# A sentence's v moved, and the gate's product behind one more expert chunk, in a fused attention and expert kernel

## The chip, the cores and the metric

The kernel runs on one core of a Trainium2 chip. The metric is the device time of one execution in microseconds (us). TensorE (PE) multiplies matrices into PSUM, a small accumulator memory; VectorE (DVE), ScalarE (ACT) and GpSimd (POOL) work elementwise; SyncE (SP) only issues transfers (DMA). Each engine runs its own list of instructions in order, and waits at an instruction whose input or buffer is not ready. Transfers issued by POOL go through one queue (q0), those issued by SP through another (q1); both are served by the same 16 DMA engines. POOL's transfers convert from float32 to 16-bit numbers on the way, SP's do not.

## The reference

For each of 8 sentences: attention in 8 heads over 576 positions with head size 64, where a position sees itself and the 63 before it; then one expert network for the whole sentence, chosen by a gate.

```python
scores = scale * np.matmul(q, k.transpose(0, 1, 3, 2))
mask = (rel >= 0) & (rel < window)          # window 64
attn = softmax of the masked scores
x = attn @ v, heads side by side            # (8, 576, 512)
...
logits = x.mean(axis=1) @ w_gate            # one row per sentence
e = argmax(logits); gate_w = softmax(logits)[e]
out = gate_w * (np.maximum(x @ w1[e], 0.0) @ w2[e])
```

q, k, v are float32 (8, 8, 576, 64); w1 is (8, 512, 1024) and w2 (8, 1024, 512) in float32. The expert of a sentence is known only when its attention is done, and only then can its weights be loaded: per sentence 2 MB each of w1 and w2 as float32.

## The kernel before

A sentence `b` is two half-sentences (units) of four heads, so there are 16 units `t`. The main loop has one step per unit, from step 4 to step 19; units 0 to 3 and the first expert chunks stand ahead of it in a hand-written start. All instructions are recorded in program order, so the order of the code is the order on each engine.

In a step `t` PE turns q and k of the next unit (`transpose_qk`), computes scores of this unit in three pieces (`scores(t, c)`: ACT takes the exponential, DVE multiplies with the band's 0/1 mask in `mask_out`), multiplies with v (`values`, two pieces; the row sums come out as a 65th column, and DVE divides in `norm`), and turns the finished x of the unit before (`transpose_x`; ACT copies it to `xT` and takes the sums over the sentence as it does, DVE forms the gate's partial sums `gpart` of them). Between these stand chunks of the expert of an earlier sentence, called in portions by `experts(pace)`: eight up-chunks (`expert_up`, 8 matmuls into `php`, ReLU and gate weight on ACT into `hT`), then five down-chunks (`expert_down`, into `pso`, copied to `ob` by DVE or ACT, stored by SP).

PSUM is given out in four buffers in turn (`psum`, four of 4 KB per partition): a new product waits until whoever reads the product four allocations earlier is done.

At an even step the sentence before is complete. `next_gate` then issues the gate's product (`gl`, one small matmul with ones that adds over partitions), five small DVE instructions (`glog`, `gmx`, `graw`, `eidx`, `gnm`) that find the expert's number, and on POOL a register load of it, the load of w1, q and k of a later unit, w2, and the load of a later sentence's v. POOL holds one queue of this, in order. Two w1 buffers and two w2 buffers exist. The first two sentences' w1 is loaded in two halves, the first of which suffices for the first four up-chunks; the others whole.

v of a sentence is loaded by SP into one of three buffers (`load_v`), 36 blocks of 128 rows in (partition, block, 64) layout. To place it in time a one-element write by POOL goes ahead of it: a memset, which waits only for the buffer, or a copy of an element of some tile, which also waits for that tile. DVE casts v to 16 bits for each unit: `cast_part` "whole" into `va`, then "low" and "high", the same shifted by half a block, into `vb`; `cast_v` does all three.

In the kernel before, the fourth sentence's v (b = 3) comes in two transfers: 20 blocks in the start, 16 blocks at step 5 behind the landing of the second half of the second sentence's w1 (`load_rest`). The fifth's (b = 4) is issued at the end of step 5. Sentences 5 to 7 are issued in `next_gate` of steps 6, 8 and 10. SP's list holds the stores of `ob` as well; `ob` has ten buffers.

In an even step `t` from 6 on the order around the gate is: `transpose_x(t - 1)`, two pieces of scores with their masks held back, one expert chunk, the gate, the two masks, the cast of the next v ("whole"), one expert chunk, the third piece of scores, the gate's weight. At step 16, the last gate, there are no scores.

## Time and profile before

| | us |
|---|---|
| median of 3 runs | 225.32 (225.25 to 226.03) |
| the profiled execution | 225.92 |
| its span, first to last instruction | 224.0 |
| PE busy in the span | 201.1 (90%) |
| ACT busy | 134.2 (60%) |
| DVE busy | 128.6 (57%) |
| share of 16 DMA engines by q0 (POOL's) | 65.3% |
| share by q1 (SP's) | 28.9% |

The span is shorter than the execution's time by 1.9 us, which lie before the first and after the last instruction. Times in rows of the profile are counted from the span's start. A row of the timeline gives start, duration, engine, line, operation and tiles, how many instructions it merges, and in brackets how long the engine stood idle before it and what ended that. A row of the chain gives start, duration and what it was. DMA rows give a queue's packets, megabytes and the time that its packets took as a share of the 16 engines, or one issue's size and the us from issue to landing.

### The profile page before, as it was taken

Reading aid. Unit: us, or ns where it says so; the run is one execution under the profiler, and the core shown is the slowest. Engines: PE = TensorE matmul, PEld = TensorE weight load, DVE = VectorE, ACT = ScalarE, POOL = GpSimd, SP = SyncE. Lnnn points to the kernel's source line nnn. Section 1 sums busy time; section 2 is a strip of 40 time slices with the busy share of each in tenths; the row PEclk is TensorE's granted clock in tenths of the full one; section 3 lists DMA queues with packets and bytes.
Section 4 is the critical chain, followed back from the end, with each engine's and each line's share of the span. In section 5 each row is a group of like instructions: output and inputs, shape, how many; then the busy total and the mean of one; then the engine's idle time right before and its main releaser. Section 6 shows DMA issues by size and latency. Waiting matters only on the chain.

```text
span 224.0 us, 6996 instructions
## 1 busy us (share of the span) xinstructions
PE 201.1 (90%) x3012; PEld 141.4 (63%) x3012; DVE 128.6 (57%) x310; ACT 134.2 (60%) x221; POOL 39.1 (17%) x69
## 2 busy tenths in 40 slices
PE   7859759999799897999999999999999998999960
PEld 2437638856586556865696658775777567569520
DVE  2538696557866665576774769395939373330120
ACT  2275695964768464785769476968495656417300
POOL 7170161053000700034000700050002000200000
PEclk9976999999999999999999999999999999999995
DMA  5999899999999999999999999999956990699141
GB/s 69 243 256 246 149 157 219 242 251 235 257 225 203 236 223 244 230 288 217 244 227 277 218 231 235 250 264 219 246 141 113 212 266 5 97 225 263 52 136 41
DMA packets 34310, 45.64 MB, mean 204 GB/s; under 512 B 7136, under 2 KB 26720, under 8 KB 34272
## 3 DMA queue, kind: packets, MB, share of 16 engines
q0 software_dynamic: 14624, 26.22, 65.3%
q1 hardware_dynamic: 18704, 18.75, 28.9%
q8 instruction: 25, 0.41, 0.7%
q10 hardware_dynamic: 944, 0.16, 0.4%
q14 instruction: 13, 0.11, 0.1%
HBM read 61.90 MB, written 9.44 MB: 318 GB/s over the span
## 4 chain that ended last, share of the span: by engine, by line
PE 64%; DMA 12%; ACT 11%; DVE 6%; issue 2%; POOL 1%; POOLq 0%
PE php L570 26%; PE pso L584 20%; DMA w1t<-in_moe_w_dram 8%; PE tp L342 6%; ACT xT L470 5%; DMA kn<-in_k_dram 4%; PE op L425 4%; ACT hT L574 4%; PE sp L382 2%; PE pso L601 2%; ACT pt L397 2%; DVE x L441 1%; PE tp L462 1%; DVE vb L311 1%; PE gl L501 1%
## 5 line engine op out<-in xcount | busy, mean ns | idle before, releaser
L570 PE MATMUL php<-xT,w1t 128*128 128x288 f16 x512 | 70.0, 287 | 3.4 <-DMA w1t<-in_moe_w_dram 2.3
L574 ACT ACTIVATE hT<-php,gatew 128x576 f16<-128x576 f32 x64 | 47.2, 744 | 28.8 <-PE php L570 28.6
L570 PEld LDWEIGHTS <-w1t 128*128 128x128 f16 x512 | 56.0, 115 | 10.0 <-DMA w1t<-in_moe_w_dram 2.9
L584 PE MATMUL pso<-w2t,hT 128*128 128x512 f16 x256 | 60.2, 380 | 0.2
L397 ACT ACTIVATE pt<-sp 128x768 f16<-128x768 f32 x48 | 36.4, 817 | 7.5 <-PE sp L382 7.5
L584 PEld LDWEIGHTS <-hT 128*128 128x128 f16 x256 | 23.3, 98 | 26.1 <-issue 1.2
L311 DVE COPY ob<-pso 128x512 f32<-128x512 f32 x23 | 15.9, 690 | 22.9 <-PE pso L584 22.7
L441 DVE TENSOR_TENSOR x<-op,linv 128x640 f16<-128x640 f32 x32 | 26.4, 825 | 1.1
L404 DVE TENSOR_TENSOR pt<-pt,masks 128x768 f16<-128x768 f16 x42 | 22.6, 554 | 5.7 <-ACT pt L397 4.7
L355 ACT COPY dst<-tp 128x1152 bf16<-128x1152 bf16 x16 | 18.0, 1124 | 11.9 <-PE tp L342 11.7
L547 POOL DMA_DIRECT2D w1t<-in_moe_w_dram x6 | 4.4, 729 | 112.8 <-DVE pt L404 91.5
L470 ACT ACTIVATE xT<-tp 128x576 f16<-128x576 f16 x28 | 17.9, 646 | 9.2 <-PE tp L462 9.2
L425 PE MATMUL op<-vb,pt 128*64 128x65 f16 x320 | 16.2, 198 | 0.8 <-DVE ob L311 0.7
L311 DVE COPY vb<-va 64x1152 f16<-64x1152 f16 (+1 forms) x32 | 15.9, 498 | 0.5
L425 PEld LDWEIGHTS <-pt 128*64 128x64 f16 x640 | 13.9, 114 | 3.3 <-issue 2.4
L425 PE MATMUL op<-va,pt 128*64 128x65 f16 x320 | 15.9, 198 | 0.0
L382 PE MATMUL sp<-dst 64*64 64x128 bf16 (+1 forms) x672 | 14.2, 218 | 1.9 <-ACT dst L309 1.2
L382 PEld LDWEIGHTS <-dst 64*64 64x64 bf16 x672 | 10.3, 110 | 8.7 <-issue 4.5
L311 DVE CAST va<-vn 128x1152 f16<-128x1152 f32 x16 | 12.2, 763 | 6.2 <-DMA vn<-in_v_dram 6.1
L493 DVE SCALAR_TENSOR_TENSOR gpart<-wg,pooled,gpart 128x8 f32<-128x8 f32 x21 | 4.8, 226 | 18.4 <-ACT xT L470 18.1
L342 PE MATMUL tp<-ident,kn 128*64 128x128 bf16 x288 | 11.5, 227 | 1.9 <-DMA kn<-in_k_dram 1.9
L342 PEld LDWEIGHTS <-kn 128*64 128x64 bf16 x288 | 9.0, 113 | 6.0 <-issue 3.5
(74 smaller groups left out, 178.5 us busy)
## 6 DMA issues: line engine op xcount, KB each, us to landing
w2t<-in_moe_w_dram POOLq DMA_DIRECT2D x8, 1024.0 KB, 17.6
out_dram<-ob SPq DMA_DIRECT2D x31, 256.0 KB, 8.1
w1t<-in_moe_w_dram POOLq DMA_DIRECT2D x6, 1024.0 KB, 9.4
qn<-in_q_dram POOLq DMA_DIRECT2D x16, 288.0 KB, 13.2
kn<-in_k_dram POOLq DMA_DIRECT2D x16, 288.0 KB, 14.3
w1t<-in_moe_w_dram POOLq DMA_DIRECT2D x4, 512.0 KB, 8.3
out_dram<-ob SPq DMA_DIRECT2D x16, 64.0 KB, 7.3
vn<-in_v_dram SPq DMA_DIRECT2D x1, 640.0 KB, 21.1
```

The lines of the kernel that those rows point to most:

```text
L311: P(eng.tensor_copy(out=out, in_=in_))
L342: P(nc.tensor.transpose(out=tp[64 * s:64 * s + 64, ts(t, 128)], in_=src[:, s, ts(t, D)], identity=ident, tile_position=(0, 64 * s)))
L355: P(nc.scalar.copy(out=dst.rearrange("p (x r t) -> p x r t", x=2, t=NT), in_=view))
L382: P(nc.tensor.matmul(out=sp[64 * half:64 * half + 64, s, 64 * (qblk - 6 * c):64 * (qblk - 6 * c) + n], lhsT=kT[64 * s:64 * s + 64, ts(kblk ...
L397: P(nc.scalar.activation(out=pt, in_=sp[:, :, 0:384], func=AF.Exp, scale=scale))
L404: P(nc.vector.tensor_tensor(out=pt, in0=pt, in1=masks[:, c].rearrange("p s g w -> p s (g w)"), op=ALU.mult))
L425: P(nc.tensor.matmul(out=op[64 * half:64 * half + 64, xx, 65 * jj:65 * jj + 65], lhsT=pt[:, s, 64 * (g % 6):64 * (g % 6) + 64], rhs=win, s ...
L441: P(nc.vector.tensor_tensor(out=x[:, :, h0 * D:(h0 + 2) * D].rearrange("p j (x c) -> p x j c", x=2), in0=view[:, :, :, 0:64], in1=li[:, :, ...
L470: P(nc.scalar.activation(out=xT[:, kb, :], in_=tp[:, kl, 0:S], func=AF.Copy, accum_out=pooled[:, b, kb:kb + 1]))
L570: P(nc.tensor.matmul(out=php[:, sc, 0:288], lhsT=w1t[:, kb, cols], rhs=xT[:, kb, ts(sc, 288)], start=(kb == 0), stop=(kb == KB - 1)))
L574: P(nc.scalar.activation(out=hT[:, ft].rearrange("p (sc s) -> p sc s", sc=2), in_=php[:, :, 0:288], func=AF.Relu, scale=gatew[:, b:b + 1]))
L584: P(nc.tensor.matmul(out=pso[:, 0, :], lhsT=hT[:, fb, ts(mt, 128)], rhs=w2t[:, fb, :], start=(fb == 0), stop=(fb == FB - 1)))
```

## The change

Three things are moved; what is computed stays the same.

- The fourth sentence's v is loaded in one transfer in the start. The second transfer at step 5, with its copy behind w1, is gone (`load_rest`, and the `part` of `load_v`).
- The fifth sentence's v is issued in `next_gate` of step 4, between w2 and the q/k of unit 7, in place of the end of step 5.
- At steps 8, 10, 12, 14 and 16 (`easy`) the expert chunk that stood behind the gate's product stands ahead of it. The two masks follow their scores at once, and the "whole" cast stands ahead of the gate's chain too. At step 4 `cast_v(5)` moves behind the last two calls of expert chunks.

```diff
-    def load_v(b, behind=None, part=0):
+    def load_v(b, behind=None):
...
-        if part:
-            P(nc.sync.dma_start(out=vn[:, 0:part, :], in_=vv[b][:, 0:part, :]))
-        else:
-            P(nc.sync.dma_start(out=vn, in_=vv[b]))
-
-    def load_rest(b, part, behind):
-        vn = v_tiles[b]
-        P(nc.gpsimd.tensor_copy(out=vn[:, part, 0:1], in_=behind))
-        P(nc.sync.dma_start(out=vn[:, part:NM, :], in_=vv[b][:, part:NM, :]))
+        P(nc.sync.dma_start(out=vn, in_=vv[b]))
...
-    load_v(3, part=20)
+    load_v(3)
...
-            if START + 1 < t and t // 2 + 2 < B:
+            if t // 2 + 2 < B:
                 load_v(t // 2 + 2)
...
+        easy = gated and t > START + 3
...
-        if t == START + 2:
-            load_rest(3, 20, w1_parts(1)[:, 1, 0, 0:1])
...
-            scores(t, 0, not gated)
-            scores(t, 1, not gated)
+            scores(t, 0, easy or not gated)
+            scores(t, 1, easy or not gated)
         if t > START + 1:
             experts(pace)
+        if easy:
+            if ahead:
+                cast_part(t + 1, "whole")
+            experts(pace)
         if gated:
             next_gate()
-            if on:
+            if on and not easy:
                 mask_out(t, 0)
                 mask_out(t, 1)
...
-            if gated:
+            if gated and not easy:
                 cast_part(t + 1, "whole")
-        experts(pace)
+        if not easy:
+            experts(pace)
...
-        if t in (4, 5):
+        if t == START + 2:
             cast_v(t + 1)
-        if t == START + 2:
-            load_v(4)
...
         experts(pace)
         experts(pace)
+        if late:
+            cast_v(t + 1)
```

SP's list from the start to step 6, before (`vn_583` is v of the third sentence, `vn_590` of the fourth, `vn_1494` of the fifth, `vn_1596` of the sixth; `ob` are the first expert's outputs):

```order
L231 DMA vn_583<-in_v_dram 128x36x64
L229 DMA vn_590<-in_v_dram 128x20x64
L596 DMA out_0_dram<-ob_1090 128x512
L596 DMA out_0_dram<-ob_1127 128x512
L609 DMA out_0_dram<-ob_1181 64x256 x2
L596 DMA out_0_dram<-ob_1202 128x512
L596 DMA out_0_dram<-ob_1264 128x512
L236 DMA vn_590<-in_v_dram 128x16x64
L231 DMA vn_1494<-in_v_dram 128x36x64
L231 DMA vn_1596<-in_v_dram 128x36x64
```

and after (the fifth's v is `vn_1073`, the sixth's `vn_1594`):

```order
L228 DMA vn_583<-in_v_dram 128x36x64
L228 DMA vn_590<-in_v_dram 128x36x64
L228 DMA vn_1073<-in_v_dram 128x36x64
L588 DMA out_0_dram<-ob_1093 128x512
L588 DMA out_0_dram<-ob_1130 128x512
L601 DMA out_0_dram<-ob_1184 64x256 x2
L588 DMA out_0_dram<-ob_1205 128x512
L588 DMA out_0_dram<-ob_1264 128x512
L228 DMA vn_1594<-in_v_dram 128x36x64
```

The fifth's v has moved from behind the first expert's five outputs to ahead of them, right behind a whole fourth.

DVE around the gate of step 8, before (`pt` are the scores' exponentials, `va` the cast v, `gatew` the gate's weight):

```order
L493 TENSOR_SCALAR gpart_1790<-wg,pooled,gpart_1790 128x8 x2
L505 COPY glog<-gl 128x8
L507 MAX gmx<-glog 128x8
L509 MAX_INDEX graw<-gmx,glog 128x8
L510 TENSOR_SCALAR eidx<-graw 128x8
L513 TENSOR_SCALAR gnm<-gmx 128x1
L404 TENSOR_TENSOR pt<-pt,masks 128x768 x2
L311 COPY va_120<-vn 128x18x64
L404 TENSOR_TENSOR pt<-pt,masks 128x768
L529 RECIPROCAL gatew<-gsum 128x1
```

and after:

```order
L485 TENSOR_SCALAR gpart_1788<-wg,pooled,gpart_1788 128x8 x2
L396 TENSOR_TENSOR pt<-pt,masks 128x768 x2
L303 COPY va_120<-vn 128x18x64
L497 COPY glog<-gl 128x8
L499 MAX gmx<-glog 128x8
L501 MAX_INDEX graw<-gmx,glog 128x8
L502 TENSOR_SCALAR eidx<-graw 128x8
L505 TENSOR_SCALAR gnm<-gmx 128x1
L396 TENSOR_TENSOR pt<-pt,masks 128x768
L521 RECIPROCAL gatew<-gsum 128x1
```

The chain from `glog` to `gnm` has moved behind two masks and the cast; what follows it is the same.

PE at the same gate, before (the last matmul of one up-chunk, the gate's product, the first matmul of the next up-chunk):

```order
L570 LDWEIGHTS w1t_1588
L570 MATMUL php<-xT_1281,w1t_1588 128x288
L501 MATMUL gl<-gpart_1790,onesf 128x8
L570 LDWEIGHTS w1t_1588
L570 MATMUL php<-xT_1281,w1t_1588 128x288
```

and after (the last matmul of the second up-chunk, the product, the third piece of scores):

```order
L562 LDWEIGHTS w1t_1586
L562 MATMUL php<-xT_1282,w1t_1586 128x288
L493 MATMUL gl<-gpart_1788,onesf 128x8
L374 LDWEIGHTS dst
L374 MATMUL sp<-dst 64x64
```

The product stands behind both chunks that enclosed it before.

## The prediction

> **What bounds the kernel now.** First the page's busy rows, then TensorE's (PE's) instructions in order of time with what ended each idle stretch, then the chain that ended last.
>
> ```profile
> PE 201.1 (90%) x3012; PEld 141.4 (63%) x3012; DVE 128.6 (57%) x310; ACT 134.2 (60%) x221; POOL 39.1 (17%) x69
> ```
>
> ```profile
> 59.04 1.14 PE L570 MATMUL php<-xT,w1t 128*128 128x288 f16 x8 [1.00 <-ACT xT L470]
> ...
> 76.78 0.19 PE L425 MATMUL op<-vb,pt 128*64 128x65 f16 x1 [0.75 <-DVE ob L311]
> ...
> 85.46 1.17 PE L570 MATMUL php<-xT,w1t 128*128 128x288 f16 x8 [1.45 <-DMA w1t<-in_moe_w_dram]
> ...
> 96.63 0.36 PE L501 MATMUL gl<-gpart,onesf 128*128 128x8 f32 x2 [0.32 <-DVE gpart L493]
> ...
> 188.92 0.39 PE L501 MATMUL gl<-gpart,onesf 128*128 128x8 f32 x2 [0.82 <-DVE gpart L493]
> ```
>
> PE is the bound: it is busy 201.1 us of the 224.0 us span, and from the middle of the program on it stops only briefly. The change can win only what stands in such brackets, and can lose by making a new one. Two groups matter. At 76.78 and 85.46 PE waits around the load of the third expert's w1. At 96.63 and at each later gate it waits 0.32 us, at the last one 0.82, for the sums that the gate's product reads.
>
> **The early part: v3 whole, v4 beside the second w1.** The wait at 76.78 starts with VectorE (DVE): its cast stood still for the rest of v3, and `ob` (which frees PE's buffer) is behind that cast.
>
> ```profile
> 75.28 0.86 DVE L311 CAST va<-vn 128x1152 f16<-128x1152 f32 x1 [1.98 <-DMA vn<-in_v_dram]
> ...
> 73.40 12.02 DMA w1t<-in_moe_w_dram
> ```
>
> With v3 loaded whole before step 5 the cast has its data, runs at about 73.3 behind the masks, and PE's 0.75 us goes. What is late next is the third w1: 12.02 us from issue to landing, at 85.42. Without the 0.75 us PE wants it at 85.46 - 1.45 - 0.75 = 83.26. Does it land 2.2 us earlier? The DMA rows, one window each (40 to 48, 49 to 51.5, 66 to 72, 74 to 78; q0 is POOL's queue, q1 SP's; packets, MB, share of 16 engines):
>
> ```profile
> q0 software_dynamic: 917, 1.01, 72.7%
> q1 hardware_dynamic: 920, 0.94, 42.2%
> ...
> q1 hardware_dynamic: 2306, 0.59, 120.9%
> ...
> q0 software_dynamic: 874, 0.95, 91.3%
> q1 hardware_dynamic: 873, 0.22, 27.7%
> ...
> q1 hardware_dynamic: 958, 0.89, 112.0%
> q0 software_dynamic: 2, 0.01, 1.0%
> ```
>
> v2, loaded whole, moves in packets of 1 KB (0.94 MB in 920): 42.2% of 16 engines for 8 us over 920 is 59 ns each. v3, cut in two, moves in packets of 256 B: 1.209 x 16 x 2.5 us / 2306 = 21 ns each for the first 20 blocks, and 0.277 x 16 x 6 us / 873 = 30 ns for the other 16. So cut v3 costs 2560 x 21 + 2048 x 30 = 115 us of engine time, whole 1152 x 59 = 68; the difference is 47 / 16 = 2.9 us of all engines, freed ahead of the third w1. In 74 to 78, moreover, v4 alone moved while w1, issued at 73.40, got two packets through; after the change v4 is done by then. So w1 lands earlier by between 0 (if POOL's queue, slowed by v4, empties later than now) and the 2.9 us freed and more. I take 2.0 us, nearer to the freed time because the engines are filled in all these rows. PE then gets 0.75 + 1.45 less 0.2 still waited: 2.0 us. Ends: 0 and 2.2.
>
> What v4 can hurt is the second w1. Its issues, the landing of its two halves, and the chain's row in which its fifth chunk (the first of the second half) stands second:
>
> ```profile
> 47.24 1.50 POOL L544 DMA_DIRECT2D w1t<-in_moe_w_dram  x2 [12.67 <-DVE pt L404]
> ...
> w1t<-in_moe_w_dram POOLq DMA_DIRECT2D x1, 512.0 KB, 9.0
> ...
> w1t<-in_moe_w_dram POOLq DMA_DIRECT2D x1, 512.0 KB, 12.8
> ...
> 63.50 2.08 PE php L570 x16
> ```
>
> The first half lands at 56.2 and is wanted at 59.04 (PE waits there for xT, so nothing is gained by it coming sooner); the second at 60.8, wanted at 64.5. If w1 starts behind v3's end, as the 49 to 51.5 rows suggest, whole v3 takes 1.18 MB at 0.89 MB per 4 us = 5.3 us in place of 0.655 MB at 0.59 per 2.5 = 2.8: the landing moves by 2.5 us to 58.7, inside the room of 2.8. Once both queues run they take turns (917 against 920). I take no cost; ends 0 and what the first rival gives.
>
> Here a rule can be weighed. The Trainium skill (DMA: Bandwidth & Descriptors, section Queues, rings and completion order) says that each engine goes round the queues that have work, packet by packet. The 40 to 48 rows agree (917 against 920), those of 74 to 78 do not (2 against 958). By the rule alone w1 would share from the start and this term would be a cost of zero for sure; by the trace it can be shut out for a while.
>
> The marker for v4 is one more POOL instruction ahead of the q/k loads of step 7, of the memset kind, with no wait: its buffer, v1's, was cast long before. v4's issue stands ahead of the out stores on SP's queue, which have ten `ob` buffers to wait in. v3's copy behind w1 (POOL) and one SP issue go. `cast_v(5)` moves behind an `ob` copy: DVE does the same work in the other order. All these at zero; if the casts come late, PE's next row at 59.04 already has 1.00 us of cover.
>
> **The gates of steps 8 to 16.** PE's chunk fills the wait, so 0.32 us (0.82 at step 16) falls away; against that the chain of five small DVE instructions moves behind two masks and a cast. Step 8, DVE, ACT and POOL:
>
> ```profile
> 96.26 0.23 DVE L493 SCALAR_TENSOR_TENSOR gpart<-wg,pooled,gpart 128x8 f32<-128x8 f32 x1 [0.40 <-ACT xT L470]
> ...
> 96.11 1.52 ACT L397 ACTIVATE pt<-sp 128x768 f16<-128x768 f32 x2
> ...
> 97.70 0.17 DVE L510 TENSOR_SCALAR eidx<-graw 128x8 uint32<-128x8 uint32 x1
> 97.85 1.02 DVE L404 TENSOR_TENSOR pt<-pt,masks 128x768 f16<-128x768 f16 x2
> 98.78 0.75 DVE L311 CAST va<-vn 128x1152 f16<-128x1152 f32 x1
> 99.63 0.56 DVE L404 TENSOR_TENSOR pt<-pt,masks 128x768 f16<-128x768 f16 x1
> ...
> 101.43 0.70 DVE ob L311
> 102.17 1.89 PE pso L584 x8
> ```
>
> The second mask cannot begin before its exponentials end at 97.63, so it ends near 98.2, the cast near 98.9, and the chain, 0.88 us from the product's end (96.99) to `eidx` (97.87), near 99.7: `eidx` comes 1.8 us later, and with it w1's issue, w2, the q/k loads and v behind it on POOL and SP. The third mask waits for its own exponential until 99.6 anyhow, so it slips by 0.1 only. But this path, third mask, two copies, `ob`, is what PE waits for at 102.17: at steps 8 and 10 the 0.32 us are not a gain, since `ob` comes no sooner; each costs 0.1. At steps 12 and 14 one and two more up-chunks stand before that buffer is wanted, and PE keeps 0.2 and 0.3.
>
> Then w1 itself. Issues at steps 8, 10, 12 and 16, time to landing of each, and first uses in the chain, steps 8 to 16:
>
> ```profile
> 98.96 0.72 POOL L547 DMA_DIRECT2D w1t<-in_moe_w_dram  x1 [21.19 <-DVE pt L404]
> 122.86 0.75 POOL L547 DMA_DIRECT2D w1t<-in_moe_w_dram  x1 [19.55 <-DVE pt L404]
> 146.17 0.72 POOL L547 DMA_DIRECT2D w1t<-in_moe_w_dram  x1 [18.93 <-DVE pt L404]
> 191.26 0.71 POOL L547 DMA_DIRECT2D w1t<-in_moe_w_dram  x1 [21.24 <-DVE okt L621]
> ...
> w1t<-in_moe_w_dram POOLq DMA_DIRECT2D x1, 1024.0 KB, 9.7
> ...
> w1t<-in_moe_w_dram POOLq DMA_DIRECT2D x1, 1024.0 KB, 9.1
> ...
> w1t<-in_moe_w_dram POOLq DMA_DIRECT2D x1, 1024.0 KB, 10.1
> ...
> w1t<-in_moe_w_dram POOLq DMA_DIRECT2D x1, 1024.0 KB, 8.2
> ...
> 109.98 2.08 PE php L570 x16
> ...
> 133.90 1.10 PE php L570 x8
> ...
> 157.76 0.98 PE php L570 x8
> ...
> 181.96 2.08 PE php L570 x16
> ...
> 200.50 7.84 PE php L570 x64
> ```
>
> Room now: 109.98 - 108.7 = 1.3; 133.90 - 132.0 = 1.9; 157.76 - 156.3 = 1.5. A shift of 1.8 us gives a wait of up to 0.5, 0 and 0.3 to 0.6 (step 12's PE is earlier by its gain). With less ahead of it w1 needs 8.2 us, which leaves no wait at all; I take 0.2, 0 and 0.3. Step 14's issue stands about midway between 146.17 and 191.26, so even 10.1 + 1.8 us end at 180.6, before its use at 181.96: no wait. At step 16 there are no masks: PE is free at 188.10, the pulled-up chunk takes 1.1 us, the product comes 0.3 us later, and w1 at 199.7 meets a use at 200.50 - 0.82 = 199.7: gain 0.7.
>
> **Sum.** -2.0 (early), +0.1 +0.2 (step 8), +0.1 (step 10), -0.2 +0.3 (step 12), -0.3 (step 14), -0.7 (step 16): -2.5 us. The profiled execution took 225.92 us; the sum gives 223.4 for it. It stands 0.6 above the median of the runs, 225.32, so I forecast 222.8.
>
> **Rivals.**
> 1. *The second w1 is shut out by v3 and v4 one behind the other* (slower). For it: the 74 to 78 rows, where v4 had the engines alone with w1 issued. Against: whole v2 took turns with POOL's queue in 40 to 48. Price: a further 5.3 us, landing at 58.7 + 5.3 = 64.0, so PE stands 5.0 us longer at 59.04; the third w1 and v3 then cost nothing (-2.2), the gates -0.5: +2.3, 227.6. It decides against the change from a landing later than 59.04 + 2.7 = 61.7.
> 2. *The third w1 lands no earlier* because POOL's queue, shared with v4 from 50 on, empties later by what it saves afterwards: PE's 0.75 is waited at 85.46 instead. Only the gates' -0.5 is left: 224.8. For it: the engines are filled throughout, so v4 moved is v4 paid elsewhere; against it: the 2.9 us of smaller packets.
> 3. *The later gates lose*: every w1 wait at its upper end (0.5 to 0.8, 0.3, 0.6), no gain at 12, and 0.3 at 16: with the early 2.0 still about 0.8 below before, 224.5.
>
> **Chances.** Forecast 0.58 (its own range 221.6 to 224.2), first rival 0.13, second 0.15, third 0.10, the rest 0.04. 0.5% is 1.1 us, about what can be told from no change. Faster takes the forecast and a little of the third (0.60); same the second and most of the third (0.24); slower the first and the rest (0.16). Low end: all early gains and no w1 wait; high end 226.0, beyond the second and third, with the first left out.
>
> **What would show it.** Right: no idle on DVE before the cast at 75, and less than 0.5 us before the first `php` of the third expert; v packets of 1 KB only; brackets of `gl` gone; `eidx` 1.8 us later against `gpart`; `ob` still before `pso` at steps 8 and 10. Wrong: a bracket `<-DMA w1t` near 59, or several of half a microsecond or more from step 8 on.

## The result, and the profile after

The changed kernel takes 223.6 us (median of 8 runs, 222.85 to 224.54) where the kernel before takes 225.28 (8 runs, 225.05 to 226.03). The ratio is 0.9915, with a 95% interval of 0.9893 to 0.9938: some 0.9% faster. The forecast was 222.8. The profiled execution took 223.97 us with a span of 222.1, against 225.92 and 224.0.

The head of the page of after, and its rows of queues (packets, MB, share of 16 engines):

```profile
PE 200.6 (90%) x3011; PEld 142.1 (64%) x3012; DVE 128.1 (58%) x310; ACT 134.1 (60%) x221; POOL 38.9 (18%) x68
```

```profile
q0 software_dynamic: 14624, 26.22, 66.1%
q1 hardware_dynamic: 15232, 18.75, 27.8%
```

PE has the same work. What shrank is q1's: 27.8% of 222.1 us is 61.7 us of all 16 engines, where 28.9% of 224.0 were 64.7. These are about 3.0 us; the prediction worked out 2.9 from the packets' sizes. (The 256 B packets took 23 ns each where the prediction had 21 and 30, and the 1 KB packets that replace them are 1152: both its terms were some 0.6 us too large, and that cancels.) q0's time is the same (146.8 against 146.3).

To place the gain, use the eight instructions with which PE begins the up-chunks of each expert. PE's rows in order of time, before (those of the second and third expert, 59.04 and 85.46, stand in the prediction) and after:

```profile
32.53 1.54 PE L570 MATMUL php<-xT,w1t 128*128 128x288 f16 x11 [0.87 <-DMA w1t<-in_moe_w_dram]
...
109.91 1.54 PE L570 MATMUL php<-xT,w1t 128*128 128x288 f16 x11
...
133.84 1.17 PE L570 MATMUL php<-xT,w1t 128*128 128x288 f16 x8
...
157.60 1.14 PE L570 MATMUL php<-xT,w1t 128*128 128x288 f16 x8
...
181.89 1.54 PE L570 MATMUL php<-xT,w1t 128*128 128x288 f16 x11
...
200.33 1.51 PE L570 MATMUL php<-xT,w1t 128*128 128x288 f16 x11
```

```profile
32.33 1.54 PE L562 MATMUL php<-xT,w1t 128*128 128x288 f16 x11 [0.82 <-DMA w1t<-in_moe_w_dram]
...
58.29 1.17 PE L562 MATMUL php<-xT,w1t 128*128 128x288 f16 x8 [0.45 <-DMA w1t<-in_moe_w_dram]
...
83.77 1.17 PE L562 MATMUL php<-xT,w1t 128*128 128x288 f16 x8 [1.76 <-DMA w1t<-in_moe_w_dram]
...
96.61 1.67 PE L576 MATMUL pso<-w2t,hT 128*128 128x512 f16 x7 [0.27 <-ACT hT L566]
...
108.00 1.54 PE L562 MATMUL php<-xT,w1t 128*128 128x288 f16 x11
...
131.72 1.17 PE L562 MATMUL php<-xT,w1t 128*128 128x288 f16 x8
...
156.37 1.17 PE L562 MATMUL php<-xT,w1t 128*128 128x288 f16 x8 [0.76 <-DMA w1t<-in_moe_w_dram]
...
180.63 1.54 PE L562 MATMUL php<-xT,w1t 128*128 128x288 f16 x11
...
198.52 1.54 PE L562 MATMUL php<-xT,w1t 128*128 128x288 f16 x11 [0.26 <-DMA w1t<-in_moe_w_dram]
```

The differences between neighbouring rows give the time of each stretch:

| stretch (first up-chunk of one expert to that of the next) | before | after | change |
|---|---|---|---|
| 1st to 3rd: the early part | 52.93 | 51.44 | -1.49 |
| 3rd to 4th: step 8 | 24.45 | 24.23 | -0.22 |
| 4th to 5th: step 10 | 23.93 | 23.72 | -0.21 |
| 5th to 6th: step 12 | 23.76 | 24.65 | +0.89 |
| 6th to 7th: step 14 | 24.29 | 24.26 | -0.03 |
| 7th to 8th: step 16 | 18.44 | 17.89 | -0.55 |
| sum | 167.80 | 166.19 | -1.61 |

The rest of the span, before the first row and behind the last, gave 0.3 more. That rest is no part of the change: in the profiles below the first row stands between 31.6 and 33.9 us, and the time from the end of PE's last product to the end of the span differs by over 1 us. The experiments are therefore read by these stretches first, and by ratios of the whole time second.

In the early part the wait at 76.78 is gone, since DVE's cast no longer stands still for v3 (DVE's rows of after, from step 6 and then from the gate of step 8):

```profile
72.48 0.75 DVE L303 CAST va<-vn 128x1152 f16<-128x1152 f32 x1
73.15 0.68 DVE L303 COPY ob<-pso 128x512 f32<-128x512 f32 x1
...
94.56 0.23 DVE L485 SCALAR_TENSOR_TENSOR gpart<-wg,pooled,gpart 128x8 f32<-128x8 f32 x1 [0.41 <-ACT xT L462]
95.26 1.26 DVE L396 TENSOR_TENSOR pt<-pt,masks 128x768 f16<-128x768 f16 x2 [0.47 <-ACT pt L389]
...
97.78 0.17 DVE L502 TENSOR_SCALAR eidx<-graw 128x8 uint32<-128x8 uint32 x1
...
98.54 0.90 DVE L303 COPY vb<-va 64x1152 f16<-64x1152 f16 x2
```

The third w1's wait is not gone: 1.76 us at 83.77 instead of 1.45 at 85.46. At the gates the brackets of `gl` are gone too, but PE has a new one of 0.27 us behind each (96.61 at step 8), labelled with ACT's `hT`, after 0.14 at the scores in front of it, which wait for ACT too. The chain ends 3.16 us behind `gpart` (97.95 against 94.79) where it ended 1.38 behind it (97.87 against 96.49): 1.8 us later. At step 12 this shows: 0.76 us for w1 at 156.37.

DMA rows of after, for the windows that the prediction used (40 to 48, 49 to 51.5, 74 to 78):

```profile
q0 software_dynamic: 920, 1.01, 72.6%
q1 hardware_dynamic: 923, 0.95, 42.3%
...
q1 hardware_dynamic: 584, 0.60, 107.1%
q0 software_dynamic: 18, 0.01, 3.7%
...
q0 software_dynamic: 310, 0.56, 74.2%
q1 hardware_dynamic: 316, 0.53, 39.2%
```

v3 now moves in 1 KB packets (0.60 MB in 584). In 74 to 78, where v4 had shut w1 out, the two queues take turns; q0's packets there are mostly q and k of unit 8, which land at 75.89 and 78.25, and those of w1 begin at 76.1. In 49 to 51.5 the second w1, issued at 47.02, is shut out by v3 as before: the 18 packets are the last of a k issued ahead of it, from 50 to 51.5 q0 moves nothing, and w1's first packet goes at 51.9.

### The profile page after: what moved, and what is told of

Same layout as the page of the kernel before. It is cut to its first block, busy times and chain, and to the rows that moved or that the text cites. A ratio compares the mean times of both kernels' runs of the same rounds, so it can differ in the third digit from the quotient of the medians.

```text
span 222.1 us, 6992 instructions
## 1 busy us (share of the span) xinstructions
PE 200.1 (90%) x3012; PEld 141.9 (64%) x3012; DVE 127.6 (57%) x310; ACT 134.3 (60%) x221; POOL 38.8 (17%) x68
## 3 DMA queue, kind: packets, MB, share of 16 engines
q1 hardware_dynamic: 15232, 18.75, 27.8%
## 4 chain that ended last, share of the span: by engine, by line
PE 53%; DMA 25%; ACT 10%; DVE 5%; issue 2%; POOL 1%; POOLq 1%
PE php L562 24%; DMA w1t<-in_moe_w_dram 21%; PE pso L576 14%; PE tp L334 5%; DMA kn<-in_k_dram 5%; ACT xT L462 4%; PE op L417 4%; ACT hT L566 3%; ACT pt L389 3%; PE sp L374 2%; PE pso L593 2%; DVE x L433 1%; PE tp L454 1%; PE sp L361 1%; PE gl L493 1%
## 5 line engine op out<-in xcount | busy, mean ns | idle before, releaser
L303 DVE COPY vb<-va 64x1152 f16<-64x1152 f16 (+1 forms) x32 | 14.8, 462 | 0.5
L431 DVE RECIPROCAL linv<-op 128x10 f32<-128x10 f32 x32 | 6.9, 216 | 11.1 <-PE op L417 11.1
```

The costliest lines, as they stand in the source:

```text
L303: P(eng.tensor_copy(out=out, in_=in_))
```

## The experiments

Each experiment is an edit of the changed kernel, but for the second, which edits the kernel before. Its stretches in us, as in the table above (the early part in its two halves, 1st to 2nd expert and 2nd to 3rd):

| run | 1-2 | 2-3 | step 8 | 10 | 12 | 14 | 16 | ratio to before [95%] |
|---|---|---|---|---|---|---|---|---|
| before | 26.51 | 26.42 | 24.45 | 23.93 | 23.76 | 24.29 | 18.44 | 1 |
| after | 25.96 | 25.48 | 24.23 | 23.72 | 24.65 | 24.26 | 17.89 | 0.9915 [0.9893, 0.9938] |
| early part alone | 25.96 | 25.50 | 25.92 | 23.93 | 23.76 | 24.29 | 18.44 | 0.9954 [0.9925, 0.9983] |
| gates alone | 26.51 | 26.31 | 24.23 | 23.71 | 24.57 | 24.25 | 17.72 | 1.0002 [0.9979, 1.0025] |
| cast_v(5) back | 26.51 | 24.71 | 24.23 | 23.71 | 24.44 | 24.26 | 17.77 | 0.9889 [0.9852, 0.9925] |
| early part, last gate | 25.73 | 25.63 | 24.44 | 23.93 | 23.76 | 24.29 | 17.91 | 0.9928 [0.9899, 0.9956] |
| v4 back | 26.09 | 25.35 | 24.23 | 23.72 | 24.40 | 24.26 | 18.13 | one run, 222.86 us |
| v4 in the start | 25.70 | 25.70 | 24.23 | 23.71 | 24.21 | 24.25 | 17.93 | one run, 223.61 us |
| chain first | 25.91 | 25.56 | 24.36 | 23.84 | 23.69 | 24.23 | 17.82 | 0.9931 [0.9897, 0.9965] |
| unit 8 behind w1 | 25.68 | 24.01 | 27.70 | 23.71 | 24.29 | 24.25 | 18.21 | 0.9936 [0.9901, 0.9971] |
| and w2 ahead of unit 9 | 25.79 | 23.56 | 26.37 | 23.71 | 24.32 | 24.25 | 17.86 | 0.9932 [0.9904, 0.9960] |
| the same, chain first | 25.62 | 23.73 | 25.51 | 23.84 | 23.69 | 24.22 | 17.95 | 0.9869 [0.9830, 0.9908] |
| units 8 and 10 | 25.72 | 23.78 | 24.51 | 25.99 | 23.49 | 24.23 | 18.22 | 0.9860 [0.9812, 0.9907] |
| units 8 to 14 | 25.76 | 23.73 | 24.36 | 24.28 | 23.69 | 24.46 | 17.90 | 0.9884 [0.9834, 0.9935] |

In two rows one entry is larger than its waits explain: at step 8 of "early part alone" PE has no new wait, but the profile grants it a mean clock of 0.93 from 84.6 to 110.5 us; at step 8 of "unit 8 behind w1" the clock is 0.66 from 95 to 100. Before and after the change it is 1.00 on the mean from 40 to 190 us (rows below).

**The two parts apart.** First the early part without the gates, then the gates without the early part.

```diff
-        easy = gated and t > START + 3
+        easy = False
```

> The changed kernel without its gate part: the v loads and the moved cast alone. Theory (from the two traces): the early part is worth 1.5 us at the first use of the third expert's w1, limited there by w1's landing near 83.7, and the gate part is worth only 0.3 us in all (0.2 each at steps 8 and 10, a loss of 0.7 at step 12 and 0.1 at step 14, a gain of 0.7 at step 16). Then this kernel takes about 223.9, its brackets on the gate's product are back (0.32 us four times, 0.82 at the last), and there is no wait for w1 at step 12. Rival (the sum on record): early part 2.0, so 223.3, and no wait of more than 0.3 us at the third w1.

The second takes the kernel before and gives it the third bullet of the change, without the move of `cast_v(5)`.

> The kernel before with the gate part alone. Theory: 225.0 (0.3 below before), the third w1 and the rest of v3 are waited for as before (1.45 and 0.75 us), w1 at step 12 is waited for 0.5 to 0.8 us, the last gate gains 0.7. Rival (the whole gain comes from the early part): no less than 225.3. Rival (the gate part carries the gain): 224.0 or less.

The early part alone has the early gain of the whole change (51.46 against 51.44 us) and nothing at the gates, and is faster, by 0.2% to 0.8%. The gates alone gain 0.2 us each at steps 8 and 10 and 0.7 at step 16, lose 0.8 at step 12, and gain nothing in the whole time. In the sum of the stretches they gain 0.5 us, in the measured time none. So the gain that can be placed is the early part's. The early part alone took 224.6 us (12 runs) where 223.9 was expected, 0.5% below the kernel before; the whole change is 0.6% to 1.1% below it, and the two intervals overlap, so whether more than the early part reaches the whole time is not shown.

**The cast of the fifth v back in its old place.**

```diff
-        if t == START + 2:
+        if t in (4, 5):
             cast_v(t + 1)
...
-        if late:
-
-            cast_v(t + 1)
```

> The changed kernel with cast_v(5) put back ahead of the two last expert chunks of step 4. Theory: before the change the wait of 1.00 us at 59.04 was for the PSUM buffer that DVE's ob copy frees behind that cast, not for xT; so with the cast back PE waits there until about 58.9 again, for ob, and not until w1's landing at 58.24. The time stays the same as the changed kernel's within 0.3 us, because the wait at the third w1 (1.76 us) shrinks by the same 0.6: that landing sets the time. Rival (xT sets it, as the prediction said): the first php of the second expert starts as in the changed kernel, 58.3. Rival (the 0.6 us are carried to the end): 0.6 us slower than the changed kernel.

PE's rows at the second and third expert:

```profile
59.25 1.14 PE L562 MATMUL php<-xT,w1t 128*128 128x288 f16 x8 [0.99 <-ACT xT L462]
...
83.96 1.17 PE L562 MATMUL php<-xT,w1t 128*128 128x288 f16 x8 [1.01 <-DMA w1t<-in_moe_w_dram]
```

The first half is back at 26.51 us, with the bracket of before. So DVE's order alone made that bracket. But it is not `ob` that ends it, as the expectation had it. The rows of before around 59.04, then `ob` after the change:

```profile
58.45 0.69 DVE L311 COPY ob<-pso 128x512 f32<-128x512 f32 x1
...
58.79 0.20 ACT L470 ACTIVATION_READ_ACCUMULATOR xT<-tp 128x1 f32 x1
...
56.51 0.69 DVE L303 COPY ob<-pso 128x512 f32<-128x512 f32 x1
```

The product starts at 59.04, 0.05 us behind the end of ACT's work on xT and 0.10 ahead of the end of `ob`; with the cast back it is 59.25 against 59.20 and 59.35. In both traces the semaphore that it waits for is ACT's, after the change it is DVE's. The xT that ACT writes there belongs to the third sentence, and the product reads the second's, so what ACT frees is most likely the PSUM buffer of the transposed x. After the change the product then takes the buffer that `ob` frees, at 57.20, before PE comes to it. So the four buffers are not always taken in the same turn: DVE's order decided which one this product got. The move of `cast_v(5)`, which the prediction put at zero, is worth 0.55 us there. But the next half gives it back: PE comes later to the third w1 and waits 1.01 us for it instead of 1.76. Both halves together are 51.22 against 51.44: the third w1's landing sets the time here, and the cast's place at most 0.2 us of it.

**Where v4 goes.** One kernel issues the fifth's v at the end of step 5 as before, with the fourth's still whole; one issues it in the start, right behind the fourth's.

```diff
-            if t // 2 + 2 < B:
+            if START + 1 < t and t // 2 + 2 < B:
                 load_v(t // 2 + 2)
...
         if t == START + 2:
             cast_v(t + 1)
+            load_v(4)
```

> The changed kernel with v of the fifth sentence issued at the end of step 5 again; v of the fourth stays whole. Theory: the second w1 waits only for whole v3 in SP's queue, so it starts and lands as in the changed kernel (58.2, counted from an equal start), whether v4 is behind v3 or not. The third w1 lands later than in the changed kernel (v4 is in its way again) but sooner than before the change (no small packets): between 83.7 and 85.4. Rival (v4 is what delays the second w1): it lands at 56.3 again, as before the change.

```diff
-            if t // 2 + 2 < B:
+            if START + 1 < t and t // 2 + 2 < B:
...
     load_v(3)
+    load_v(4)
```

> The changed kernel with v of the fifth sentence issued right behind that of the fourth in the start, some 4 us sooner, so that both stand ready in SP's queue when the second w1 is issued. This is the first rival of the prediction made real. If w1 waits for everything that SP's queue holds ready, it starts only at 58 to 59 and lands near 63.5: a wait of about 5 us at the first php of the second expert. If it waits only for the transfer in progress (theory), it lands near 58.2 as in the changed kernel, and nothing changes by more than 0.5 us.

PE's rows at the second expert, of the first and of the second of these:

```profile
57.89 1.17 PE L562 MATMUL php<-xT,w1t 128*128 128x288 f16 x8 [0.58 <-DMA w1t<-in_moe_w_dram]
```

```profile
57.35 1.17 PE L562 MATMUL php<-xT,w1t 128*128 128x288 f16 x8 [0.20 <-DMA w1t<-in_moe_w_dram]
```

The early part takes 51.44 and 51.40 us, as after the change. The second w1 lands 11.3 and 11.0 us behind its issue, after the change 11.2. The third w1 lands 51.4 us behind the first up-chunk in both, as after the change (before it 52.9); with v4 back it had been expected later. So the place of v4 makes no difference that shows, late or early: what the early part gains comes from v3 whole. Whether that is its larger packets or its second part moved ahead of the second w1 was not tested apart; that v4, moved by as many bytes, changes nothing speaks for the packets. And the first rival falls: even with v4 directly behind v3 on SP's list (its issue begins at 45.50 us, the second w1's at 46.34), w1 lands no later. Its packets begin at 51.0, when some 60% of v3's packets are through, and do not wait for v4. How much of v4 stood in the queue by then is not shown, since SP's issue of it lasts until 52.94.

**The gates.** One kernel has the new order at step 16 only; in the other the product stays one chunk later at all five steps, but its chain stands ahead of the masks and the cast again.

```diff
-        easy = gated and t > START + 3
+        easy = t == NU
```

> The changed kernel with the gate part at step 16 alone; steps 8 to 14 as in the kernel before. Theory: the wait of 0.76 us for w1 at step 12 comes from the gate's chain standing 1.8 us later; it goes, steps 8 and 10 lose 0.2 each, step 14 gains 0.1, so 0.4 us faster than the changed kernel, about 223.2. Rival (w1 at step 12 is late because POOL's queue is behind, whatever the chain does): that wait stays and the time is 0.3 us above the changed kernel's, 223.9.

```diff
-            scores(t, 0, easy or not gated)
-            scores(t, 1, easy or not gated)
+            scores(t, 0, not gated)
+            scores(t, 1, not gated)
...
         if easy:
-            if ahead:
-                cast_part(t + 1, "whole")
             experts(pace)
...
-            if on and not easy:
+            if on:
...
-            if gated and not easy:
+            if gated:
```

> The changed kernel with the gate's product still one chunk later, but the gate's chain ahead of the two masks and the whole cast on DVE again. Two things are told apart. Step 12: if the 0.76 us for w1 come from the chain's 1.8 us (theory), they vanish here, since eidx comes only about 0.75 us later than before the change. Steps 8 and 10, each 0.2 us shorter in the changed kernel: if that is because DVE's copies into vb no longer fall into the time in which POOL issues its transfers (1.22 us for two in the kernel before, 0.90 in the changed one; theory), the copies are slow again here, ob comes late and the 0.2 us are lost; if it is the product's place on PE that gained them (rival), they stay. PE's waits for PSUM of 0.14 and 0.27 us behind the product stay in both. Time: theory 0.3 us below the changed kernel (0.7 at step 12 less 0.2 at steps 8 and 10), 223.3; rival 0.7 below.

With the chain first, PE's row at the sixth expert has no bracket, where after the change it had 0.76 us for w1:

```profile
156.14 1.14 PE L562 MATMUL php<-xT,w1t 128*128 128x288 f16 x8
```

Step 12 takes 23.69 us instead of 24.65, and 23.76 where only the last gate is changed. So the loss at step 12 is the chain behind the two masks and the cast. The whole time of the last gate alone, 223.92 us (12 runs), is nevertheless no better than the changed kernel's, where 223.2 was expected. (In the runs above with the changed gates it is between 24.21 and 24.65, so 0.45 to 0.9 us.) The gain of step 16, where nothing stands between product and chain, is kept in both.

Steps 8 and 10, however, take 24.36 and 23.84 us with the chain first, half-way between before and after. How long DVE copies `vb` there differs (of before and of this kernel; of after it stands above, 0.90 us):

```profile
100.18 1.22 DVE L311 COPY vb<-va 64x1152 f16<-64x1152 f16 x2
```

```profile
99.32 1.40 DVE L303 COPY vb<-va 64x1152 f16<-64x1152 f16 x2
```

In both, POOL issues its transfers of w1, q, k and w2 at that moment (from 98.96 and from 98.26 us on); after the change the first is issued at 99.01, when the first of the two copies is through. This is taken up at the end.

**The third w1.** After the change PE waits longest, 1.76 us, for the third w1. On POOL's queue q and k of unit 8 stand ahead of it, issued at step 5 and not needed until step 7. The next kernel issues them behind it.

```diff
+        if u == 8:
+            P(nc.gpsimd.dma_start(out=kn, in_=kv[u]))
         P(nc.gpsimd.dma_start(out=qn, in_=qv[u]))
...
-        P(nc.gpsimd.dma_start(out=kn, in_=kv[u]))
+        if u != 8:
+            P(nc.gpsimd.dma_start(out=kn, in_=kv[u]))
...
             load_w1(b)
+            if t == START + 3:
+                load_qk(8)
...
-        if t % 2 == 1 and t + 3 < NU:
+        if t % 2 == 1 and START + 2 < t and t + 3 < NU:
             load_qk(t + 3)
```

> The changed kernel with q and k of unit 8 issued behind the third expert's w1, k first, in place of step 5. Theory: the third w1 stands in POOL's queue behind these two (1.2 MB read) and so lands at 83.7; ahead of them it lands near 81, before PE wants it at 82.0, and the wait of 1.76 us goes; k of unit 8 then lands near 83.3, before it is wanted at 84.6. The first use of the third w1 comes 1.7 us sooner. Of this 1 to 1.7 us reach the end, the rest going to w1 of later sentences (step 12's wait grows): 222.0 to 222.6. Rival (the DMA engines are filled and what is taken from one transfer is waited for at another): k8 or w2 is waited for in its place and the time stays within 0.3 us of the changed kernel's.

```profile
81.52 1.17 PE L565 MATMUL php<-xT,w1t 128*128 128x288 f16 x8 [0.19 <-DMA w1t<-in_moe_w_dram]
...
96.16 1.89 PE L579 MATMUL pso<-w2t,hT 128*128 128x512 f16 x4 [2.08 <-ACT gex L522]
```

Of the wait 0.19 us are left, and the stretch is shorter by 1.47 us. But 2.08 us are waited at the same expert's first down-chunk. The label names ACT's `gex`, which ends at the same moment; but the weight load that stands ahead of this product is labelled with w2 (idle for 2.21 us until 96.16), and the third w2, issued at 75.81 behind four q and k transfers, landed 20.3 us later, at 96.11. The next kernel puts w2 ahead of unit 9's q and k, and the one after it has the chain first besides.

```diff
-            if START + 1 < t < NU - 3:
+            if START + 3 < t < NU - 3:
                 load_qk(t + 3)
             load_w2(b)
+            if t == START + 3:
+                load_qk(t + 3)
```

> The changed kernel with three transfers of the third expert's stage in another order: k and q of unit 8 go behind the third w1 instead of ahead of it, and the third w2 goes ahead of q and k of unit 9 instead of behind them (with unit 8 alone moved, the wait for the third w1 fell from 1.76 to 0.19 us, but w2 then landed at 96.11, and PE waited 2.08 us for it). Theory A (the third w1's landing is what sets the time in this stretch, and the w2 wait came only from four q and k transfers ahead of it): wait for the third w1 0.2, none over 0.3 at the second product of the third expert; from the first product of the second expert to that of the third expert about 24.0 us as with unit 8 alone, and the next interval back from 27.7 to about 24.3; the kernel takes 1.5 us less than the changed kernel's 223.6, so about 222.1. Theory B (the bytes in this stretch fill the queue so that what is gained in one place is waited for in another): some transfer of units 8 to 10 or the third v is late, a wait of over 0.8 us appears within the third expert, and the time stays within 0.5 us of 223.6.

> The kernel of the run above, and besides the gate's chain back ahead of the two masks and the cast, the product still one expert chunk behind x (as in the run that put the chain first, which lost the step-12 wait). Theory A: both act apart from each other: the third w1's wait is gone as above (24.0 us to the third expert's first product), steps 8 and 10 as with the chain first (24.36 and 23.84), and step 12 at 23.7 instead of 24.65 since the w1 there is not waited for; so 1.5 + 0.8 us less than the changed kernel's 223.6, about 221.3, and ratio to the kernel before about 0.982. Theory B: with the third w1 no longer waited for, PE arrives sooner at the later w1 transfers and waits there again for what was saved: intervals of steps 8 to 16 sum to more than 115.0 us (with the chain first 113.9), and the time is 222.5 or more.

PE's rows of the first, then of the second:

```profile
96.35 0.69 PE L337 MATMUL tp<-ident,kn 128*64 128x128 bf16 x18 [0.39 <-DMA kn<-in_k_dram]
...
107.63 1.54 PE L565 MATMUL php<-xT,w1t 128*128 128x288 f16 x11 [1.64 <-DMA w1t<-in_moe_w_dram]
```

```profile
107.05 1.54 PE L565 MATMUL php<-xT,w1t 128*128 128x288 f16 x11 [1.11 <-DMA w1t<-in_moe_w_dram]
```

Third w1 and third w2 come in time now, and the stretch up to the third expert is 1.8 to 1.9 us shorter than after the change; most of it is waited for at the fourth w1, 1.64 and 1.11 us where there had been no wait. Theory B held in its substance, though its wait stands one expert further on than it said: 223.75 us (12 runs) without the chain first, as after the change. With the chain first it is 222.54 us (6 runs); steps 8 to 16 sum to 115.21 us, over the 115.0 that tells the theories apart.

The last two kernels carry the same order on: unit 10's q and k behind the fourth w1, then also units 12's and 14's behind the fifth and sixth, each time w2 ahead of the other unit (`DEFER` is then `(8, 10, 12, 14)`).

```diff
+    DEFER = (8, 10)
...
             load_w1(b)
+            if t + 2 in DEFER:
+                load_qk(t + 2)
...
-            if START + 1 < t < NU - 3:
+            if START + 1 < t < NU - 3 and t + 2 not in DEFER:
                 load_qk(t + 3)
             load_w2(b)
+            if START + 1 < t < NU - 3 and t + 2 in DEFER:
+                load_qk(t + 3)
...
-        if t % 2 == 1 and t + 3 < NU:
+        if t % 2 == 1 and t + 3 < NU and t + 3 not in DEFER:
             load_qk(t + 3)
```

> The kernel of the run before (unit 8's q and k behind the third w1, chain first), and the same for unit 10 at step 8: its k and q go behind the fourth w1, and the fourth w2 ahead of unit 11's q and k. In the run before, PE waited 1.11 us at 107.05 for the fourth w1, which landed at 107.00 to 107.58 in four kernels that issued it anywhere between 95.54 and 99.01. Theory A (on POOL's queue a transfer lands when the bytes issued ahead of it are through; the 4.6 us of unit 10's q and k are ahead of it for no need): the fourth w1 lands at 102.4 to 104.5, its wait is gone, the interval from the third to the fourth expert falls from 25.51 to 24.4, and since nothing is taken from the queue, the fifth w1 still lands at about 130.0, where PE then arrives at about 129.8: a wait of 0.2 to 0.5 there or at the sixth, so 0.6 to 0.9 us gained of 1.1, about 221.8. Theory B (DMA as a whole is too slow there, whatever the order): the fourth w1 lands no earlier than 106.5, and the time stays at 222.5.

> The same at all four steps: the q and k of units 8, 10, 12 and 14 each go behind the w1 that is issued next, and that step's w2 ahead of the other unit's q and k. Theory A: no w1 from the third to the sixth is waited for (each has 4.6 us fewer bytes ahead of it), the 1.1 us of step 8 is kept to the end, and the kernel takes about 221.4 us, ratio to the kernel before about 0.982. What speaks against it: units 9, 11 and 13 then land 4.6 us later than before; unit 9's k did so 0.39 us too late in one run and in time in the other, so waits of 0.1 to 0.4 us may stand at each of steps 8, 10 and 12. Theory B (order gains nothing, the queue is simply full): PE waits at steps 8 to 12 for other transfers, w2 or k, 1 us or more in sum, and the time is 222.3 or more.

PE's rows of the first, then of the second:

```profile
123.14 0.69 PE L338 MATMUL tp<-ident,kn 128*64 128x128 bf16 x18 [0.84 <-DMA kn<-in_k_dram]
...
133.87 1.17 PE L566 MATMUL php<-xT,w1t 128*128 128x288 f16 x8 [0.97 <-ACT pt L393]
```

```profile
106.51 1.54 PE L566 MATMUL php<-xT,w1t 128*128 128x288 f16 x11
...
121.09 0.69 PE L338 MATMUL tp<-ident,kn 128*64 128x128 bf16 x18 [0.37 <-DVE pt L400]
...
130.79 1.17 PE L566 MATMUL php<-xT,w1t 128*128 128x288 f16 x8
```

With units 8 and 10 moved, the wait at the fourth w1 is gone, as theory A had it, but not by A's landing of 102.4 to 104.5: w1 lands at 107.83, past the 106.5 of theory B. In this profile PE's first up-chunk stands 1.7 us later than in the run before; counted from the first up-chunk w1 lands 0.85 us sooner than there (73.96 against 74.81), just as PE comes to it. Instead, 0.84 us for a k and 0.97 at the fifth expert are waited (the second labelled with ACT's `pt`, its weight load with w1, which landed at 133.83 us), more than A's 0.2 to 0.5. With all four moved no wait above 0.4 us is left between the third and the seventh expert, and the seven stretches sum to 164.18 us, the least of all kernels here (after the change 166.19). Its time, 223.06 us (6 runs), is nevertheless no better than 222.54 and 222.80 of the two kernels ahead of it: their intervals overlap widely, and in its profile the 24.04 us from the start of the eighth expert to the end of the span hold 1.0 more than the 23.03 of the kernel with 222.54, all of it behind PE's last product. So its waits are as theory A had them and its time is as B had it (222.3 or more), and whether the last reordering is worth anything in the whole time stays open. The three kernels with the chain first and reordered loads are 1.2% to 1.4% faster than the kernel before. Against the changed kernel that is 0.3% to 0.6% more, measured at other times; the intervals overlap, so this further gain is likely rather than shown.

What these rows have behind them is one view: the busy time and DMA share of a long window in the middle, of before and of after (window, its length, five engines' busy time, clock, share of the DMA engines, GB/s):

```profile
40.00:190.00 150.00, 143.40 (x2259) 103.21 (x2252) 98.33 (x227) 101.35 (x176) 23.04 (x36) 1.00 1.03 223
```

```profile
40.00:190.00 150.00, 144.40 (x2264) 105.70 (x2258) 98.14 (x232) 102.96 (x179) 22.71 (x35) 1.00 1.02 222
```

The DMA engines are filled throughout, and PE is busy 96% of it. Reordering their work brings one transfer sooner and others later, for the most part by as much: of the kernels with the chain first, the best reordering has 1.2 us less in the sum of the stretches (164.18 against 165.40). A wait for a transfer is then no reserve of its own length: the two kernels that moved only q, k and w2 took the third w1's 1.76 us nearly or wholly away and came out at 0.9936 and 0.9932 of the kernel before, no faster than the changed kernel's 0.9915.

Why did the fourth w1 of the last kernel land no sooner than 105.75 us, where 102.4 to 104.5 was expected? Its DMA rows from 97 to 98.5 and from 98.5 to 104.5 us:

```profile
q1 hardware_dynamic: 290, 0.48, 84.3%
q0 software_dynamic: 9, 0.04, 29.2%
...
q0 software_dynamic: 292, 1.05, 96.4%
q1 hardware_dynamic: 40, 0.07, 3.0%
```

Issued at 96.33, with nothing ahead of it on POOL's queue once unit 9's k had landed at 96.60, its first packet goes at 98.05, 1.7 us after the issue. Then it had the engines nearly to itself for six microseconds. The late start is hardly SP's doing: before the change, w1 issued at 168.56 with no packet on any queue from then on has its first at 170.02, after 1.5 us. So there is a floor under the landing that the order of POOL's queue doesn't lower: one and a half to two microseconds until it starts, and six for its 1.05 MB.

## Why the prediction was right, and where not

- **The sum.** -2.5 us was forecast; the stretches give -1.61, the profiled execution -1.95, the medians -1.7. The direction, the early part as its main source and the range held. Both larger terms came out smaller than predicted. Two of the signs that the prediction names went against it: a wait for w1 near 59 (0.45 us at 58.29), and 1.76 us before the third expert where it allowed 0.5.
- **Early part, -2.0 predicted, -1.49 measured.** The price of the packets was right (2.9 us of all engines against about 3.0), and the third w1 lands 1.5 us sooner, counted from the first up-chunk (51.39 against 52.89 us behind it), within the ends of 0 and 2.2 but below the 2.0 taken. The mechanism held, the size of that landing was off. "0.2 still waited" was wrong by far: 1.76 us are waited, since PE comes sooner as well, for two reasons that the prediction had smaller or not at all. The wait behind DVE's cast at 76.78 was worth 1.25 us instead of 0.75: PE reached the down-chunks behind that `op` product 18.33 us after the second expert's first row before and 17.17 after, the one behind the next `op` 20.22 and 18.97. Only the first idle stretch was in the bracket; the others were too short to show.
- **`cast_v(5)` at zero, and the second w1 "wanted at 59.04".** This step failed. PE did wait for ACT's xT there, but only while the cast stood ahead of `ob` on DVE; with the cast back the wait is back. That an order on DVE can change which PSUM buffer a product takes was not in the working. So the move costed at zero was worth 0.55 us, and the second w1's landing, at 58.24 (58.7 predicted), was then wanted at 57.84, not at 59.04: it is waited for 0.45 us. None of this moved the time by more than 0.2 us, since the third w1 comes next.
- **First rival, the second w1 shut out by v3 and v4.** It did not happen, and not even with v4 issued directly behind v3. That w1 waits for most of whole v3 was right (no packet of it until 51.9, while q1 moved 584 in 49 to 51.5). The Trainium skill's rule of turns packet by packet (DMA: Bandwidth & Descriptors, section Queues, rings and completion order) holds in three of the windows, 40 to 48, 66 to 72 and now 74 to 78 of after, and fails in 49 to 51.5 of after, as it did in 74 to 78 of before. From that rule the prediction took that this landing would cost nothing; it moved by 2.2 us, from 9.0 to 11.2 behind the issue.
- **Second rival, the third w1 no earlier.** It fell for the change: w1 is 1.5 us sooner, most likely since packets were really saved, not only moved. What the rival says, that a transfer moved is a transfer paid elsewhere, is what the later experiments showed of reordering, for the most part.
- **Gates, -0.5 predicted, -0.12 measured.** `eidx` came later by the predicted 1.8 us. At step 12 the term for w1 was mis-sized: 0.3 taken, 0.76 measured, since w1 again took 10.4 us to land and not 8.2. At steps 8 and 10 the sign was wrong: 0.2 us gained at each, no loss; `ob` is no longer waited for. At step 14 the 0.3 was taken back by the waits of 0.14 and 0.27 us behind ACT that replaced the one for the sums. Step 16 gave 0.55 of 0.7, because w1 is waited for 0.26 us. That the sum of the gates came out near is partly luck: steps 8 and 10 were 0.8 us better than predicted and step 12 0.8 worse.
- **Third rival.** The gates' loss was real at step 12 only; the gates alone measure 1.0002 [0.9979, 1.0025], not a loss.

## What to carry to other kernels

Where PE and the DMA engines are both filled, a wait for a transfer does not tell what removing it is worth: less DMA work (larger packets) shortens the time, while another order mostly moves the wait to the next transfer. Measure a stretch between two fixed instructions of PE rather than adding up brackets. A releaser's name says who ended the wait, not why: the wait for ACT's xT came and went with an order on DVE, and twice a wait for a weight's landing carried the name of an ACT instruction that ended at the same moment, where the weight load's own row named the transfer. A small chain on which a large load depends is best kept ahead of bulk work on its engine where that load is waited for: at step 12 this was worth 0.9 us, at steps 8 and 10, where it is not, it cost 0.1 each.

## What the runs showed beside this

- **DVE's copies beside POOL's issues.** From 60 us on, every `vb` copy of before, of after and of the kernel with the chain first that overlapped none of POOL's transfer issues took 0.43 to 0.46 us. Of the copies that overlapped one, 7 of 9 took 0.50 to 0.70 us in before and 5 of 9 with the chain first, but 0 of 6 after the change. So the overlap goes with the longer copies without being enough for them, and what tells the two kinds apart was not found. It fits the 0.2 us gained at steps 8 and 10 (before 1.22 us for the pair, after 0.90, with the chain first 1.40 and half the gain lost), but that this is their cause is not shown.
- **A new transfer on POOL's queue can start late beside SP's.** From its issue to its first packet w1 takes 1.4 to 1.5 us with nothing else moving (168.56 and 191.26 of before). Beside SP's queue it took 4.1 to 4.9 us at two places (47.24 and 73.40 of before, 47.02 of after), while SP's v took 83% to 113% of the engines, but only 1.5 to 1.6 at three others, where SP's queue took 91% to 103% (122.86 and 146.17 of before, 145.95 of after). What tells these apart was not found. Once both run they take turns, 920 to 923.
- **The end of the program varies by itself.** In five profiles (before, after, and the last three kernels) PE's last product ends 16.0 to 16.1 us behind the start of the eighth expert, and the span 6.7 to 7.9 us later, whatever the kernel: over half a per cent that no edit here touched.
